# Zero fills of a decode kernel's cache gradients: the source rows, 32 partitions four apart, become 16 partitions eight apart

## Chip, cores and metric

One core of a Trainium2 chip. The time is the device time of one execution in microseconds; a kernel's figure is the median of several executions. A profile comes from one further execution, whose own time is given beside its span (first to last instruction).

## What is computed

The reference is one decode step of a transformer block, forward and backward: a layer norm, attention of one new token over the last W = 4096 positions of a key and value cache of Sk = 32768 positions, a gated bilinear feed-forward part, and the gradients of nine inputs. Cut to what matters here:

```python
def _A_ref(x, k_cache, v_cache, wq, wo):
    B, Sq, D = x.shape                       # 1, 1, 448
    Hq, Dh = 16, 256
    Hkv, Sk = k_cache.shape[1], k_cache.shape[2]   # 8, 32768
    W = min(4096, max(256, Sk // 4))         # 4096
    q = (x @ wq).reshape(B, Sq, Hq, Dh) ...
    k = jnp.repeat(k_cache[:, :, Sk - W:, :], rep, axis=1)
    v = jnp.repeat(v_cache[:, :, Sk - W:, :], rep, axis=1)
    scores = jnp.einsum("bhqd,bhkd->bhqk", q, k) * (Dh ** -0.5)
    p = _softmax(scores, axis=-1)
    o = jnp.einsum("bhqk,bhkd->bhqd", p, v)
    ...

x = A_x
h = x + _A_ref(_layernorm(x, axis=-1), A_k_cache, A_v_cache, A_wq, A_wo)
h2 = h + _B_ref(_layernorm(h, axis=-1), B_w_gate, B_w_up, B_w_down)

_out, _vjp = jax.vjp(_f, A_x, A_k_cache, A_v_cache, A_wq, A_wo, B_w_gate, B_w_up, B_w_down)
_grads = _vjp(grad_out)
```

The two largest outputs are the gradients of the caches, `out_2` and `out_3`, each (1, 8, 32768, 256) in bf16. Only the last 4096 positions of a head have a gradient; the first 28672 are zeros, and they have to be written. These zeros are 16 regions (8 heads, K and V) of 14336 KB.

## The kernel before

**Zeros.** Each region is written by one DMA out of SBUF, called a fill, which reads the same zeroed rows again and again. `rows_of(src, n)` takes every fourth partition of a tile, 32 rows in all, and repeats each n times by a stride of zero (line 244). A fill's destination is cut into 32 equal stretches, one for each row.

- The two *early* fills (lines 254 and 255) read `Z_early`, which is the tile `pair`, cleared by a memset at the start (line 71): 32 KB a row, 28 times. SyncE issues them behind the first loads, which it also issues (lines 122, 123 and 212 to 217): the projection weights, K and V of the first three heads and V of head 3. GpSimd waits for both fills (line 256) before V of heads 5 and 6 is loaded into `pair`.
- The fourteen *late* fills read `Z_late`, which is the tile `home`: 16 KB a row, NZ = 28 times. `home` is at first V of head 0 (line 67). When head 0's part of the forward pass has read it, `clear_rows` (line 289) zeroes every fourth partition by one AND with a mask that is 0 in the rows to be cleared and all ones in the others (`keep_i`, built in lines 148 to 152 from an identity matrix). The 96 other partitions keep V of head 0 for the backward pass.
- `fill_late` (line 261) issues the late fills on SyncE's queue `ZQ`, two in flight (DEEP = 2): before a fill SyncE waits for the one two places earlier. After the last it waits for all (lines 284 to 287).
- The fill of region 3 (UNEVEN) is cut: 22 of the 28 repeats go as usual; the last 192 pieces of 16 KB go in six small transfers that start from given rows (line 275), four of them issued by GpSimd.

**The rest.** The forward pass goes head by head (`scores`, then `moments`, lines 401 to 414), with loads of later heads on ScalarE's queue `LD`. Then come the output projection and the feed-forward part with their gradients (lines 432 to 570). The backward pass goes through the heads in the order 6, 1, 3, 4, 5, 0, 7, 2 (line 669): per head it reads V, builds 2 MB each of K's and V's gradient in SBUF and stores both on ScalarE's queue (line 712), while GpSimd computes and stores the weight gradients.

In the third round of that loop (it == 2) all of `home` is copied into another place by VectorE (line 714), and the 32 partitions that had been cleared are loaded again from the cache (line 715), so that the copy holds V of head 0 whole for the round of head 0.

## Time and profile before

| | us |
|---|---|
| median of three runs (784.61 to 786.02) | 785.4 |
| profiled execution | 784.5 |
| its span, first to last instruction | 782.7 |
| PE busy | 474.3 |
| DVE busy | 386.1 |
| ACT busy | 197.9 |
| POOL busy | 189.9 |

PE is the matrix engine TensorE, DVE is VectorE, ACT ScalarE, POOL GpSimd, SP SyncE. Transfers run on 16 DMA engines, which serve all queues: q1 is SyncE's, q10 ScalarE's, q0 GpSimd's. The page gives each queue's packets, bytes in MB and the time of its packets as a share of 16 engines' span. The mean granted TensorE clock of the execution was 0.766 of full speed.

### The profile page before, as it was taken

What the parts mean: (1) busy time and instruction counts of PE and PEld (TensorE: products, weight loads), DVE (VectorE), ACT (ScalarE), POOL (GpSimd) and SP (SyncE); (2) the same over time, 40 slices, a digit from 0 to 9 for tenths busy, and PEclk for the clock granted to TensorE, in tenths of its full rate; (3) what the DMA queues carried; (4) which work ended last, traced back from release to release, by engine and by line L of the source; (5) the groups of instructions that cost most, each with busy time, mean ns of one, the idle gap of its engine ahead of it and who ended that gap; (6) DMA issues with size and microseconds to landing.
All of it is one profiled execution on the core that took longest, in us unless ns stands there. A gap on an engine that the chain in (4) does not pass through costs nothing.

```text
span 782.7 us, 6390 instructions
## 1 busy us (share of the span) xinstructions
PE 474.3 (61%) x2166; PEld 203.4 (26%) x2184; DVE 386.1 (49%) x1090; ACT 197.9 (25%) x309; POOL 189.9 (24%) x102
## 2 busy tenths in 40 slices
PE   1999999999689992522233598533687906502200
PEld 0444444444344441200012134211233302201000
DVE  8158545464027753104378627582468504796400
ACT  1251332323440000001011026431555503510300
POOL 7000001000000000000000096762828565590000
PEclk9999999999968996655555699955589555755555
DMA  9999999999999999999999999999999999999998
GB/s 376 430 424 428 429 432 417 424 428 428 430 430 431 423 427 427 430 430 429 432 432 428 433 429 427 427 427 412 431 426 414 425 418 430 428 432 431 429 429 353
DMA packets 23698, 331.96 MB, mean 424 GB/s; under 512 B 1774, under 2 KB 2802, under 8 KB 4946
## 3 DMA queue, kind: packets, MB, share of 16 engines
q1 hardware_dynamic: 14826, 250.43, 75.3%
q10 hardware_dynamic: 5320, 57.61, 17.4%
q0 software_dynamic: 3520, 23.51, 7.2%
q8 instruction: 17, 0.28, 0.1%
q14 instruction: 15, 0.12, 0.0%
HBM read 50.96 MB, written 280.59 MB: 424 GB/s over the span
## 4 chain that ended last, share of the span: by engine, by line
PE 41%; DMA 18%; DVE 16%; issue 3%; another core or an unknown queue 2%; ACT 2%; DVEq 0%; ACTq 0%; POOLq 0%
PE M_t L384 11%; DMA out_dram<-arena 11%; PE rows_ps L321 6%; PE tr_ps L318 6%; PE ok_ps L388 5%; PE d_ps L702 4%; DVE arena L710 2%; DVE arena L523 2%; DVE pair L729 2%; DVE arena L709 2%; DMA arena<-in_A_wo_dram 2%; DMA arena<-in_A_k_cache_dram 2%; PE dqb_ps L580 2%; DMA arena<-in_B_w_down_dram 2%
## 5 line engine op out<-in xcount | busy, mean ns | idle before, releaser
L380 DVE TENSOR_SCALAR arena<-arena,p_f 128x256 bf16<-128x256 bf16 x512 | 110.4, 282 | 38.4 <-PE M_t L384 21.0
L318 PE MATMUL tr_ps<-ident_f,arena 128*128 128x128 f32 x448 | 85.0, 318 | 58.1 <-DMA arena<-in_A_v_cache_dram 31.4
L321 PE MATMUL rows_ps<-arena,vpad 128*16 128x512 bf16 x256 | 88.1, 438 | 9.3 <-ACT arena L675 3.6
L337 ACT COPY arena<-tr_ps 128x1024 bf16<-128x1024 bf16 x64 | 63.7, 1013 | 98.5 <-PE tr_ps L318 84.6
L318 PEld LDWEIGHTS tr_ps<-ident_f,arena 128*128 128x128 f32 x448 | 55.3, 158 | 104.1 <-issue 74.5
L709 DVE CAST arena<-d_ps 128x512 bf16<-128x512 f32 x64 | 44.0, 688 | 66.0 <-PE d_ps L702 65.7
L702 PE MATMUL d_ps<-arena 32*128 32x512 bf16 x256 | 46.5, 514 | 49.1 <-DVE arena L710 41.8
L384 PE MATMUL M_t<-arena 128*128 128x512 bf16 x308 | 73.5, 380 | 1.9 <-DVE arena L380 1.5
L706 ACT CAST arena<-d_ps 128x512 bf16<-128x512 f32 x64 | 37.9, 591 | 83.3 <-PE d_ps L702 79.6
L597 POOL TENSOR_SCALAR arena<-dh_bc,oX_f 128x448 bf16<-128x448 bf16 x32 | 44.5, 1399 | 29.5 <-DMA out_dram<-arena 29.3
L710 DVE CAST arena<-d_ps 128x512 bf16<-128x512 f32 x64 | 43.5, 680 | 14.2 <-DMA out_dram<-arena 14.2
L707 ACT CAST arena<-d_ps 128x512 bf16<-128x512 f32 x64 | 38.4, 600 | 23.8 <-DMA out_dram<-arena 23.8
L388 PE MATMUL ok_ps<-arena 128*32 128x512 bf16 x208 | 43.3, 380 | 0.3 <-issue 0.3
L417 POOL DMA_DIRECT2D arena<-in_A_wo_dram x1 | 0.6, 569 | 166.3 <-PE ok_ps L388 166.3
L675 ACT COPY arena<-tr_ps 128x1024 bf16<-128x1024 bf16 x32 | 32.6, 1024 | 28.9 <-PE rows_ps L321 19.3
L384 PEld LDWEIGHTS <-arena 128*128 128x128 bf16 x320 | 29.7, 98 | 36.5 <-issue 4.3
L597 POOL TENSOR_SCALAR arena<-arena,xT 128x4096 bf16<-128x4096 bf16 x3 | 31.8, 10615 | 26.3 <-DMA out_dram<-arena 26.3
L477 PE MATMUL r_ps<-arena,X2pad 128*4 128x448 bf16 x24 | 10.4, 570 | 39.6 <-DMA arena<-in_B_w_up_dram 23.4
L702 PEld LDWEIGHTS <-arena 32*128 32x128 bf16 x256 | 10.4, 96 | 87.2 <-DVE arena L710 43.9
L597 POOL TENSOR_SCALAR arena<-pair,xT 128x1792 bf16<-128x1792 bf16 x6 | 28.7, 4791 | 12.8 <-DMA out_dram<-arena 12.8
L323 DVE COPY arena<-rows_ps 16x512 f32<-16x512 f32 x16 | 10.8, 677 | 42.5 <-PE rows_ps L321 42.3
L384 PE MATMUL M_t<-arena,pair 128*128 128x512 bf16 x124 | 30.2, 404 | 0.4 <-issue 0.2
(237 smaller groups left out, 589.8 us busy)
## 6 DMA issues: line engine op xcount, KB each, us to landing
out_dram<-home SPq DMA_DIRECT2D x13, 14336.0 KB, 89.4
out_dram<-arena ACTq DMA_DIRECT2D x16, 2048.0 KB, 27.8
out_dram<-pair SPq DMA_DIRECT2D x2, 14336.0 KB, 90.5
out_dram<-home SPq DMA_DIRECT2D x1, 11264.0 KB
arena<-in_A_k_cache_dram ACTq DMA_DIRECT2D x5, 2048.0 KB, 19.1
arena<-in_A_k_cache_dram SPq DMA_DIRECT2D x3, 2048.0 KB, 24.4
arena<-in_A_v_cache_dram SPq DMA_DIRECT2D x3, 2048.0 KB, 29.7
arena<-in_A_v_cache_dram ACTq DMA_DIRECT2D x3, 2048.0 KB, 33.5
```

Source lines behind the costliest of these rows:

```text
L318: nc.tensor.transpose(tr_ps[:, i, :], X_sb[:, 4 * q + i, :].bitcast(f32), ident_f[:])
L321: nc.tensor.matmul(rows_ps[:], lhsT=pad[:, e, 16 * q:16 * q + 16], rhs=XT.rearrange("p (n e) -> p n e", e=2)[:, :, e], start=(q == 0 and e ...
L337: sT_ps = dots(K_of[g], KT_slot, vpad[g % 2], rows1, ps_c, "cols", lambda q, XT, ps: nc.scalar.copy(out=XT, in_=ps))
L380: nc.vector.tensor_scalar(out=pK[:, i, hh, :], in0=K_sb[:, t, :], scalar1=p_f[:, 8 * i + c, hh:hh + 1], scalar2=None, op0=ALU.mult)
L384: nc.tensor.matmul(M_ps[vh], lhsT=V_sb[:, t, vh * 128:(vh + 1) * 128], rhs=pK[:, i, :, :].rearrange("p h d -> p (h d)"), start=(t == 0), s ...
L388: nc.tensor.matmul(ok_ps[32 * k:32 * (k + 1), :], lhsT=ppad[g % 2][:, t:t + 2, :].rearrange("p t h -> p (t h)"), rhs=X_sb[:, t:t + 2, :].r ...
L597: nc.gpsimd.tensor_scalar(out=buf[:, off:off + n], in0=src, scalar1=col, scalar2=None, op0=ALU.mult)
L702: nc.tensor.matmul(d_ps[:, qi].rearrange("p w d -> p (w d)"), lhsT=rm[32 * q:32 * (q + 1), l, :], rhs=Rs[32 * q:32 * (q + 1), :], start=Tr ...
L706: nc.scalar.copy(out=stV[:, t:t + 2, :], in_=d_ps[:, :, 0, :])
L707: nc.scalar.copy(out=stK[:, t:t + 2, :], in_=d_ps[:, :, 1, :])
L709: nc.vector.tensor_copy(out=stV[:, t:t + 2, :], in_=d_ps[:, :, 0, :])
L710: nc.vector.tensor_copy(out=stK[:, t:t + 2, :], in_=d_ps[:, :, 1, :])
```

## The change

The number of rows becomes a constant, ZP = 16, and their distance ZS = 128 // ZP = 8. All fills read partitions 0, 8, 16 ... 120 in place of 0, 4, 8 ... 124, and each row is repeated twice as often: NZ is 56, and the early fills repeat 56 / 2 = 28 times over 16 rows of 32 KB each with stretches twice as long. The mask clears 16 partitions of `home` and keeps 112; the reload of line 715 fetches 16 rows in place of 32. The six small transfers keep their pieces and start from rows of the new set.

```diff
-NZ = (Sk - W) * Dh // (32 * ZW)
+ZP = 16
+ZS = 128 // ZP
+NZ = (Sk - W) * Dh // (ZP * ZW)
...
-    nc.vector.reduce_sum(out=keep_f[:], in_=ident_f[:, 0:128:4], axis=AX)
+    nc.vector.reduce_sum(out=keep_f[:], in_=ident_f[:, 0:128:ZS], axis=AX)
...
-        return src[0:128:4].unsqueeze(1).to_broadcast([32, n, src.shape[1]])
+        return src[0:128:ZS].unsqueeze(1).to_broadcast([ZP, n, src.shape[1]])
...
-        fill_with(reg.rearrange("(p n f) -> p n f", p=32, f=ZE), rows_of(Z_early, NZ * ZW // ZE), esem, "early")
+        fill_with(reg.rearrange("(p n f) -> p n f", p=ZP, f=ZE), rows_of(Z_early, NZ * ZW // ZE), esem, "early")
...
-                odd = reg.rearrange("(r f) -> r f", f=ZW)[22 * 32:]
-                reg = reg[0:22 * 32 * ZW]
-                n = 22
+                odd = reg.rearrange("(r f) -> r f", f=ZW)[44 * ZP:]
+                reg = reg[0:44 * ZP * ZW]
+                n = 44
                 at = 0
-                for e, base, rows, queue in ((3, 0, 8, nc.gpsimd), (2, 12, 2, nc.gpsimd), (3, 20, 13, nc.gpsimd), (8, 64, 13, nc.gpsimd), (4, 0, 5, ZQ), (1, 0, 1, ZQ)):
+                for e, base, rows, queue in ((3, 0, 8, nc.gpsimd), (2, 3, 2, nc.gpsimd), (3, 5, 13, nc.gpsimd), (8, 8, 13, nc.gpsimd), (4, 0, 5, ZQ), (1, 0, 1, ZQ)):
                     fill_with(odd[at:at + e * rows].rearrange("(e n) f -> e n f", e=e),
-                              Z_late[base:base + 4 * e:4].unsqueeze(1).to_broadcast([e, rows, ZW]), zsem[j] if queue is ZQ else psem, "fills", queue)
+                              Z_late[ZS * base:ZS * (base + e):ZS].unsqueeze(1).to_broadcast([e, rows, ZW]), zsem[j] if queue is ZQ else psem, "fills", queue)
...
-            for dst, src in [(reg.rearrange("(p n f) -> p n f", p=32, f=ZW), rows_of(Z_late, n))]:
+            for dst, src in [(reg.rearrange("(p n f) -> p n f", p=ZP, f=ZW), rows_of(Z_late, n))]:
...
-                LD.dma_start(out=ar(S[3], 16 * KB)[0:128:4], in_=A_v_cache[0, 0, Sk - W:, :].rearrange("(p t) d -> p (t d)", t=T)[0:128:4])
+                LD.dma_start(out=ar(S[3], 16 * KB)[0:128:ZS], in_=A_v_cache[0, 0, Sk - W:, :].rearrange("(p t) d -> p (t d)", t=T)[0:128:ZS])
```

## The prediction

> **What bounds the kernel now.** I read the slices of the page first, then the queues and the DMA issues, then what SyncE and the other engines wait for, then windows of single stages, and last the chain.

> The slices over the span (DMA: mean busy share of 16 DMA engines in tenths; GB/s: what they moved):
> ```profile
> DMA  9999999999999999999999999999999999999998
> GB/s 376 430 424 428 429 432 417 424 428 428 430 430 431 423 427 427 430 430 429 432 432 428 433 429 427 427 427 412 431 426 414 425 418 430 428 432 431 429 429 353
> DMA packets 23698, 331.96 MB, mean 424 GB/s; under 512 B 1774, under 2 KB 2802, under 8 KB 4946
> ```
> The DMA engines are full from the first slice to the last: the time is bytes over rate, 331.96 MB at 424 GB/s being 782.9 us against a span of 782.7. The compute engines live inside that (PE is busy 61%).

> The queues and the issues of the fills:
> ```profile
> q1 hardware_dynamic: 14826, 250.43, 75.3%
> ...
> HBM read 50.96 MB, written 280.59 MB: 424 GB/s over the span
> ...
> out_dram<-home SPq DMA_DIRECT2D x13, 14336.0 KB, 89.4
> out_dram<-arena ACTq DMA_DIRECT2D x16, 2048.0 KB, 27.8
> out_dram<-pair SPq DMA_DIRECT2D x2, 14336.0 KB, 90.5
> ```
> q1 is SyncE's queue. The sixteen fills are 16 x 14336 KB = 234.9 MB of the 332. One engine moves on q1 250.43 MB / (0.753 x 782.7 us x 16) = 26.56 GB/s, so a 16 KB piece of a fill takes 617 ns and all fills cost 234.9 MB / (16 x 26.56 GB/s) = 552.7 us of the 782.7. The other 230 us are loads and stores.

> Who waits for the fills (engine, line, what it waited for: us in total, times, longest):
> ```profile
> SPq L247 <- DMA out_dram<-home: 555.9, 12, 71.6
> SPq L286 <- DMA out_dram<-home: 98.2, 2, 54.2
> ```
> SyncE always has two fills in flight and waits for the older; its last wait ends the program. So the pace of a fill is the pace of the kernel.

> Windows of three stages (start and end, length, busy time of PE, PEld, DVE, ACT, POOL, granted clock, DMA share, GB/s): loads alone, then almost only a fill, then fills with stores:
> ```profile
> 5.00:40.00 35.00, 21.75 (x95) 10.26 (x95) 15.04 (x29) 7.49 (x9) 10.38 (x5) 1.00 1.00 428
> 210.00:250.00 40.00, 33.48 (x128) 15.57 (x131) 17.75 (x76) 9.29 (x16) 0.00 (x0) 0.74 1.00 429
> 700.00:750.00 50.00, 8.60 (x48) 3.05 (x48) 27.30 (x40) 9.32 (x17) 4.47 (x2) 0.50 1.01 430
> ```
> Loads read HBM and write 128 partitions, fills read 32 partitions and write HBM, and both stop at the same 428 to 430 GB/s. The ceiling is therefore on what they share: the DMA engines, or the doors between these engines and SBUF.

> **The change, part by part.** *Instructions.* Every fill keeps its 14336 KB, its 16 KB pieces (32 KB for the two early ones) and their number, 896 or 448; SyncE still issues once per fill. The sum that makes the mask (line 149) reads 16 columns instead of 32; it took 200 ns once, so under 0.2 us, beside full DMA. The AND of line 291 and the copy of line 714 keep their shape. Nothing here is moved past a queue and no wait is added.

> *The reload of head 0* (line 715, ScalarE's queue) falls from 512 to 256 KB. 0.262 MB at 424 GB/s is 0.62 us of all DMA engines: -0.6 us, since the engines are never idle. It is issued at 530.49, just ahead of the two stores of line 712, which land that much sooner too.

> *The pace of a fill.* This is the whole question. Now 32 partitions give 429 GB/s in the fill-only window, 13.4 GB/s each on average; afterwards 16 must give 26.8 each, or the fill slows. No row of the trace has an SBUF side narrower than those 32 rows that runs long enough by itself. Lower bound of the cost: the engines alone are the ceiling and a piece stays at 617 ns, 0 us. Upper bound: the ceiling is at the doors, a door belongs to a set of partitions, and half of the doors are no longer used; two engines then share one door, a piece takes 2 x 617 = 1234 ns while both fill, a fill runs at 234.9 MB / 1105.4 us = 212 GB/s and all fills cost up to 552.7 us more. I take the upper price: it is a row's measured pace per source partition kept as it is, while the lower one needs every source row to give twice what any row shows it giving.

> [...]

> *What of the doubled cost is hidden.* While one engine of a pair moves a load, its partner has the door alone. At the one end both engines turn to loads and stores together, nothing overlaps, and the span is 782.7 + 552.7 - 0.6 = 1334.8 us. At the other end the shared doors are never idle: 17,920 KB (18.35 MB) of loads stand ahead of the first fill on q1, 18.35 MB / 428 GB/s = 42.9 us; then the fills take 2 x 552.7 = 1105.4; and the stores, 280.59 - 234.9 = 45.7 MB, leave through the same doors, 45.7 / 424 = 107.8 us. Together 1256.1. I take the middle, 1295.5, as the loads of a head come to all sixteen engines at once and the alternation of two queues lets part of them slip in between.

> *What else would be late.* The wait of POOL (line 256) for both early fills moves from 127 us to about 43 + 4 x 34.5 = 181, and V of heads 5 and 6 is loaded that much later; K, V and weight loads share their engines with slower pieces. The chain says how much compute hangs on transfers:
> ```profile
> PE 41%; DMA 18%; DVE 16%; issue 3%; another core or an unknown queue 2%; ACT 2%; DVEq 0%; ACTq 0%; POOLq 0%
> ```
> Even if the 18% (141 us) doubled and 54 us came on top for POOL, compute would be through at some 980 us, under fills that last to 1256 or more. So this costs nothing, and the last 300 us would be fills alone.

> *Sum.* 782.7 - 0.6 + 513.4 (the middle of 474.0, which is 1256.1 - 782.1, and 552.7) = 1295.5 us of span. The profiled execution took 784.5 us, 1.8 around its span, and the median of the runs is 785.4, 0.9 above it: 1298 us.

> **The rivals.**
> *Not slower: the engines are the ceiling.* One mechanism: a door can give two engines their 26.56 GB/s at the same time, so any 16 rows are as good as 32. It decides from the point where a door gives 53 GB/s. Then only the reload is left: 784.8 us (785.4 - 0.6). For it: each engine shows the same pace whatever queue or direction it serves. Against it: that pace is equally what a door of one engine's width would give, and the change asks the rows for something no stage has asked.
> [...]

> *Fewer engines.* The sixteen rows are dealt to eight engines only, which then carry all fills: 2 x 552.7 for these, and their 229 us of other traffic in series, 1334.8 + 2.7 = 1337 us. The busy share of DMA would fall to about 5 tenths once compute is through. Against it: the reading of 32 rows fills all sixteen now, and sixteen rows leave one for each.

> *A door with some room to spare.* If it gives a pair one and a half engines' pace, a piece costs 4/3: 552.7 / 3 = 184 more, 782.7 + 184 + 2.1 = 969 us. Against it: nothing in the slices shows a rate above 433.

> **How the numbers follow.** Shared doors 0.76, engines the ceiling 0.13, eight engines 0.06, some room 0.05. The measurement tells about 0.2% (1.6 us) from no change; the 0.6 us of the second case lies below that, so of its 0.13 I give 0.11 to the same and 0.02 to faster. Slower has the rest, 0.87. The time is that of the likeliest, 1298. The range holds the first and the third case: from 1180 (the 1256 + 2.7 of perfect overlap, less 6% if a shared door gives a little more than one engine's pace) to 1370 (1337 and 2.5% for what sharing loses). The two cases below it, 0.18 together, are left out; the end at 784.8 belongs to one of them.

> **What would show it.** In the changed profile: GB/s of the slices near 212 wherever only fills run, thus in the last quarter above all, with the DMA share still at 9 (pieces take longer, the engines don't rest); the loads-only first slices unchanged at about 428; SyncE's wait at line 247 near twice 556; fills landing some 140 us after issue in place of 89.4 where nothing else runs; compute over by 980 us and the end with SyncE's wait at line 286. A GB/s row that stays near 424 with a span near 782 makes the forecast wrong, and the engines the ceiling; a DMA share of 5 in the tail means eight engines; slices near 320 mean room to spare.

## The result and the profile after

The changed kernel takes 1416.5 us (median of 6 runs, 1414.2 to 1421.5) against 784.9 beside it: 1.804 times as long, 95% interval 1.802 to 1.807. The direction and the mechanism came as forecast, the size did not: 1298 was said, with 1370 as the upper end.

The slices over the changed kernel's span (one slice is now 35.3 us), and its queues and issues:

```profile
span 1412.4 us, 6390 instructions
...
PE   4999764895302136832272600510200000000000
...
DMA  9999999999999999999999889966994999999991
GB/s 399 285 264 258 287 342 310 204 260 324 226 224 224 245 205 204 230 256 233 253 218 264 278 275 202 223 228 193 226 249 123 201 205 203 204 204 202 206 201 55
...
q1 hardware_dynamic: 14826, 250.43, 75.3%
q10 hardware_dynamic: 5304, 57.35, 12.7%
q0 software_dynamic: 3520, 23.51, 5.7%
...
out_dram<-home SPq DMA_DIRECT2D x13, 14336.0 KB, 145.6
out_dram<-arena ACTq DMA_DIRECT2D x16, 2048.0 KB, 70.7
out_dram<-pair SPq DMA_DIRECT2D x2, 14336.0 KB, 140.4
```

The reader is to see four things. The number of packets and bytes on q1 is the same to the last digit, so the transfers are the same ones. The DMA row stays at 9 over most of the span while GB/s falls to 204 wherever nothing but fills is left: the engines are busy, each piece takes longer. Against the forecast, the DMA row does not stay at 9 everywhere: slices 23 to 31 and the last one have holes. And a 2 MB store of a head's gradient lands after 70.7 us in place of 27.8.

Windows of the changed kernel (columns as before): loads alone, then fills alone.

```profile
5.00:40.00 35.00, 21.91 (x99) 10.59 (x99) 15.01 (x29) 8.11 (x9) 10.38 (x5) 1.00 1.01 429
1105.00:1365.00 260.00, 0.00 (x0) 0.00 (x0) 0.00 (x0) 0.00 (x0) 0.00 (x0) 0.50 0.99 204
```

Loads are untouched at 429 GB/s. Fills run at 204 with all engines busy (0.99), 12.75 GB/s for each engine, so a 16 KB piece takes 1285 ns against 617 before.

SyncE's waits (what for, us in total, times, longest) say the same of whole fills:

```profile
SPq L249 <- DMA out_dram<-home: 1110.5, 12, 159.7
SPq L288 <- DMA out_dram<-home: 108.5, 2, 71.5
```

Line 249 is line 247 of before; the 555.9 us have become 1110.5, twice as much within 0.2%.

**Where the 629.7 us of span went.** The share of each queue in sixteen engines' span, times the span, is engine time. Beside q1's 75.3% the page of before gives:

```profile
q10 hardware_dynamic: 5320, 57.61, 17.4%
q0 software_dynamic: 3520, 23.51, 7.2%
```

| engine time, us | before | after | more |
|---|---|---|---|
| q1: fills and first loads | 589.4 | 1063.5 | 474 |
| q10: ScalarE's loads and stores | 136.2 | 179.4 | 43 |
| q0: GpSimd's loads and stores | 56.4 | 80.5 | 24 |
| no packet at all (span less the shares) | under 1 | 88 | 88 |

q8, which carries instructions, has 0.1% on both sides. The time without a packet is called dry time below.

### The profile page after: what moved, and what is told of

It reads as the page before. It is cut to its first block, busy times and chain, and to the rows that moved or that the text cites. A ratio compares the mean times of both kernels' runs of the same rounds, so it can differ in the third digit from the quotient of the medians.

```text
span 1412.4 us, 6390 instructions
## 1 busy us (share of the span) xinstructions
PE 488.3 (35%) x2166; PEld 208.2 (15%) x2184; DVE 396.6 (28%) x1090; ACT 198.3 (14%) x309; POOL 191.6 (14%) x102
## 3 DMA queue, kind: packets, MB, share of 16 engines
q1 hardware_dynamic: 14826, 250.43, 75.3%
HBM read 50.69 MB, written 280.59 MB: 235 GB/s over the span
## 4 chain that ended last, share of the span: by engine, by line
PE 24%; DMA 21%; another core or an unknown queue 15%; DVE 9%; issue 2%; ACT 1%; SPq 0%; DVEq 0%; ACTq 0%; POOLq 0%
DMA out_dram<-arena 9%; PE M_t L386 6%; DMA arena<-in_A_k_cache_dram 5%; PE tr_ps L320 4%; PE rows_ps L323 4%; PE ok_ps L390 3%; PE d_ps L704 2%; DMA arena<-in_B_w_down_dram 2%; DMA arena<-in_A_v_cache_dram 1%; DVE pair L731 1%; DMA arena<-in_B_w_up_dram 1%; DMA arena<-in_A_wo_dram 1%; DVE arena L711 1%; DVE arena L712 1%
## 5 line engine op out<-in xcount | busy, mean ns | idle before, releaser
L320 PE MATMUL tr_ps<-ident_f,arena 128*128 128x128 f32 x448 | 89.3, 331 | 136.9 <-DMA arena<-in_A_v_cache_dram 95.9
L599 POOL TENSOR_SCALAR arena<-arena,xT 128x4096 bf16<-128x4096 bf16 x3 | 35.7, 11888 | 54.3 <-DMA out_dram<-arena 54.3
L679 DVE COPY arena<-tr_ps 128x1024 bf16<-128x1024 bf16 x32 | 22.5, 704 | 14.4 <-PE tr_ps L320 14.0
## 6 DMA issues: line engine op xcount, KB each, us to landing
out_dram<-home SPq DMA_DIRECT2D x13, 14336.0 KB, 145.6
out_dram<-arena ACTq DMA_DIRECT2D x16, 2048.0 KB, 70.7
out_dram<-pair SPq DMA_DIRECT2D x2, 14336.0 KB, 140.4
arena<-in_A_k_cache_dram ACTq DMA_DIRECT2D x5, 2048.0 KB, 32.3
arena<-in_A_k_cache_dram SPq DMA_DIRECT2D x3, 2048.0 KB, 24.1
arena<-in_A_v_cache_dram SPq DMA_DIRECT2D x3, 2048.0 KB, 29.6
arena<-in_A_v_cache_dram ACTq DMA_DIRECT2D x3, 2048.0 KB, 53.0
```

The costliest lines, as they stand in the source:

```text
L320: nc.tensor.transpose(tr_ps[:, i, :], X_sb[:, 4 * q + i, :].bitcast(f32), ident_f[:])
L599: nc.gpsimd.tensor_scalar(out=buf[:, off:off + n], in0=src, scalar1=col, scalar2=None, op0=ALU.mult)
```

## The experiments

**Sixteen rows, 32 to 92 by four.** The changed kernel with rows counted from Z0:

```diff
-ZS = 128 // ZP
+Z0 = 32
+ZS = 4
+ZR = slice(Z0, Z0 + ZP * ZS, ZS)
...
-    nc.vector.reduce_sum(out=keep_f[:], in_=ident_f[:, 0:128:ZS], axis=AX)
+    nc.vector.reduce_sum(out=keep_f[:], in_=ident_f[:, ZR], axis=AX)
...
-        return src[0:128:ZS].unsqueeze(1).to_broadcast([ZP, n, src.shape[1]])
+        return src[ZR].unsqueeze(1).to_broadcast([ZP, n, src.shape[1]])
...
-... Z_late[ZS * base:ZS * (base + e):ZS] ...
+... Z_late[Z0 + ZS * base:Z0 + ZS * (base + e):ZS] ...
...
-LD.dma_start(out=ar(S[3], 16 * KB)[0:128:ZS], in_=...[0:128:ZS])
+LD.dma_start(out=ar(S[3], 16 * KB)[ZR], in_=...[ZR])
```

> Sixteen rows as in the changed kernel, but partitions 32, 36 ... 92 in place of 0, 8 ... 120. Shared doors (two engines read through one door when their rows lie 32 apart, and rows that differ in their place within 32 or lie on the two sides of 64 have doors of their own): every engine has a door for itself, 611 to 617 ns a piece, 424 GB/s, about 784 us, that is the kernel before less the 0.6 us of the reload. Number of rows (a partition hands out no more than 13 to 14 GB/s): as slow as the changed kernel, about 1412 us.

784.8 us against 785.5 beside it, ratio 0.9993 (0.9984 to 1.0002). A window with almost only a fill:

```profile
210.00:250.00 40.00, 33.11 (x153) 15.74 (x156) 18.77 (x81) 10.25 (x18) 0.00 (x0) 0.88 1.01 431
```

Sixteen rows give 431 GB/s, each of them 27. That ends the rival of the number of rows, and any that says sixteen rows are narrow: only where they lie differs from the changed kernel. The destinations and their sixteen stretches are the same too, so the loss is not on the side of HBM.

**Sixteen rows, 0 to 60 by four.** As above with Z0 = 0.

> Sixteen rows, partitions 0, 4 ... 60: the same count and spacing as rows 32 to 92, but every row has a partner 32 away. Shared doors: a piece at 1220 to 1280 ns, fills alone at about 204 GB/s, 1330 to 1420 us. Spacing (rows eight apart are the trouble, four apart are not): about 784 us. Number of rows: about 1412 us, the same as shared doors; the run with rows 32 to 92 tells these two apart.

1323.7 us, ratio 1.685 (1.681 to 1.689), a little below the range of shared doors. Same count, same spacing, 32 partitions lower, and the pace is half. Its fills alone, in the last quarter of the slices:

```profile
DMA  9999999999999999999999999979978999999994
GB/s 399 306 252 280 257 305 342 258 202 298 307 223 225 225 243 203 204 226 262 240 291 242 276 342 263 256 279 298 235 253 210 206 204 201 204 204 205 200 204 189
```

204 GB/s again. Spacing is out: what rows 32 to 92 have and these do not is rows on both sides of partition 64. Near the end the trace shows the sharing itself:

```profile
1295.00:1315.00 20.00, 0.00 (x0) 0.00 (x0) 0.00 (x0) 0.00 (x0) 0.00 (x0) 0.50 0.50 215
```

Half of the engines have ended (0.50), and the others move 215 GB/s, more than all sixteen did: 27 for each engine instead of 12.75, as if each now had a door to itself.

**Thirty-two rows, 0 to 62 by two.** ZP = 32, Z0 = 0, ZS = 2, 28 repeats, with the cut fill of region 3 as in the kernel before.

> Thirty-two rows as in the kernel before, but partitions 0, 2 ... 62, which by the door theory lie at eight doors. Shared doors: fills at half pace, 1330 to 1420 us. Number of rows: as before, about 785 us.

1330.3 us, ratio 1.694 (1.690 to 1.697), though the number of rows is that of the kernel before. Fills alone, and the queues:

```profile
1120.00:1290.00 170.00, 0.00 (x0) 0.00 (x0) 0.00 (x0) 0.00 (x0) 0.00 (x0) 0.50 0.99 205
...
q1 hardware_dynamic: 14826, 250.43, 81.3%
q10 hardware_dynamic: 5320, 57.61, 11.5%
q0 software_dynamic: 3520, 23.51, 5.7%
```

With q8's 0.1% the shares leave 1.4% of 1328.0 us, so only some 19 us are dry here.

**Sixteen rows, 0 to 15.** Z0 = 0, ZS = 1.

> Sixteen rows side by side, partitions 0 to 15, in groups of four that have one door. Shared doors: four engines to a door, a piece at 2440 to 2560 ns, fills alone at some 102 GB/s, 2250 to 2600 us. If a fixed cost of narrow sources were the cause (half pace whatever the rows, unless they are spread as 32 to 92): about 1330 to 1412 us.

2459.2 us, a single run. Fills alone:

```profile
1700.00:2400.00 700.00, 0.00 (x0) 0.00 (x0) 0.00 (x0) 0.00 (x0) 0.00 (x0) 0.50 0.99 102
```

Half of 204 with all engines busy: 2570 ns a piece, four times 617 within 5%. The cost does not follow the number of rows: sixteen of them gave 431, 204 and 102 GB/s, thirty-two 429 and 205. At the 26.9 GB/s that each of the last eight engines moved with rows 0 to 60 (215 / 8), sixteen, eight and four doors would give 430, 215 and 108. So I count sixteen, eight and four doors, a shared one at 25.5 GB/s (204 / 8 and 102 / 4); the count is read off the paces. What the expectation for rows 32 to 92 says of doors fits rows four apart: no sharing between places within 32 or between the two sides of 64 (431 GB/s), sharing once every row has a partner 32 away (204). Rows two apart and side by side share beyond that (205 and 102), so a place within 32 is not always a door of its own.

**The reload by itself.** In the kernel before:

```diff
-LD.dma_start(out=ar(S[3], 16 * KB)[0:128:4], in_=...[0:128:4])
+LD.dma_start(out=ar(S[3], 16 * KB)[0:128:8], in_=...[0:128:8])
```

> The kernel before with the reload of head 0's values cut from 32 to 16 rows (0, 8 ... 120), so sixteen cleared rows stay zeros in the copy and the gradients that use them are left wrong. This is the saving of the change by itself: 0.262 MB at 424 GB/s is 0.6 us, 784.8 in place of 785.4, a ratio of 0.999. If the reload lay on a chain of its own and not only on the DMA engines, more than 2 us would go.

784.7 against 785.5, ratio 0.9988 (0.9979 to 0.9997). The interval ends just below one, so a small gain is likely; the 0.9992 of 0.6 us lies in it and in that of rows 32 to 92 (0.9993), and the intervals are too wide to say more.

**The early fills alone.** In the kernel before, where an early fill repeats its 32 KB rows 14 times (not 28, as its description ahead has it), 28 times after the edit:

```diff
-        fill_with(reg.rearrange("(p n f) -> p n f", p=32, f=ZE), rows_of(Z_early, NZ * ZW // ZE), esem, "early")
+        fill_with(reg.rearrange("(p n f) -> p n f", p=16, f=ZE), Z_early[0:128:8].unsqueeze(1).to_broadcast([16, NZ * ZW // ZE * 2, ZE]), esem, "early")
```

> The kernel before, with the two early fills alone reading sixteen rows eight apart; the fourteen late ones and the reload stay. Shared doors: 2 of 16 fills at half pace, 552.7 x 2/16 = 69 us at most, less what loads hide in the first 180 us: 840 to 855 us. If the late load of two heads' values (GpSimd's wait for the early fills) stopped the forward pass beyond that, over 860; if the half pace came only from the tile the late fills read, 785.

841.6 us, ratio 1.073 (1.070 to 1.075). The slices (21 us each) and GpSimd's wait:

```profile
GB/s 382 427 267 210 293 273 238 288 301 399 429 429 429 424 429 427 427 429 431 430 434 427 436 428 425 428 429 416 428 417 429 415 428 430 431 432 427 428 428 337
...
POOL pair L210 <- POOLq L256: 177.7, 1, 177.7
```

The slower pace is there as long as the early fills run (down to 210 GB/s in the fourth slice) and gone with them (429 from the eleventh on). They cost 56.8 us of the 69.1 that two doubled fills would cost with nothing hidden, so 12 us (18%) slipped in between loads. GpSimd waits 177.7 us for them in place of 111.8, and nothing comes of it: later slices are back at the rates of before.

**Four fills in flight.** In the changed kernel, to find the 88 us without packets:

```diff
-DEEP = 2
+DEEP = 4
```

> The changed kernel with four fills in flight instead of two. In the changed kernel the packets fill 93.8% of sixteen engines' span, so 1324 us of work and 88 us without any. Theory: engines fall out of step, and SyncE issues the next fill only when the slowest engine has ended the one two places earlier, so the fast ones run dry. Then four in flight take away the dry stretch about 1060 to 1100 us and part of the tail: 1330 to 1385 us. Rival: some engines simply have more work at their doors, so that they end late whatever is queued: within 10 us of 1412, the dry time only moved to the end.

1421.6 us, ratio 1.8125 to the kernel before (1.809 to 1.816): no gain. My theory fell, the rival held. The slices:

```profile
DMA  9999999999999999999999998898849999999921
GB/s 400 284 263 256 293 333 313 204 259 328 222 225 226 241 203 204 232 259 231 252 225 275 270 259 245 211 263 258 270 117 205 204 203 205 203 204 203 198 51 47
```

The tail is longer: two slices (71 us) at about 50 GB/s, and the shares of the queues leave 102 us dry in place of 88. A window in this tail, and one in that of the changed kernel:

```profile
1350.00:1400.00 50.00, 0.00 (x0) 0.00 (x0) 0.00 (x0) 0.00 (x0) 0.00 (x0) 0.50 0.25 51
...
1380.00:1410.00 30.00, 0.00 (x0) 0.00 (x0) 0.00 (x0) 0.00 (x0) 0.00 (x0) 0.50 0.13 54
```

Here four engines (0.25 of 16) are left with 51 GB/s, 12.75 each, the half pace, as two shared doors at 25.5 would give. In the changed kernel two are left with 54, 27 each, the full pace. So some engines end late with four fills in flight as with two; that with two part of this shows earlier, as SyncE waiting for the slowest, fits the holes but is not shown.

**Without the heads' stores.** In the changed kernel:

```diff
-            for o_ap, st_ in ((out_3, stV), (out_2, stK)):
-                LD.dma_start(out=o_ap[0, g, Sk - W:, :].rearrange("(p t) d -> p t d", t=T), in_=st_)
```

> The changed kernel without the sixteen 2 MB stores of the heads' gradients (33.6 MB, left unwritten). Theory: these stores leave through the same doors and put the engines out of step; without them 33.6 MB / 16 / 26.56 GB/s = 79 us of engine time go and most of the 88 dry us with them, 1245 to 1285 us. Rival (they do not matter for the dry time): 79 us at most, 1330 us or more, with DMA slices below 9 as before.

1239.0 us, ratio 1.579 (1.576 to 1.582) to the kernel before, 177 us less than the changed kernel, a little below the range given. The slices and queues:

```profile
DMA  9999999999999999999999999999999999999994
...
q1 hardware_dynamic: 14826, 250.43, 86.9%
q0 software_dynamic: 3520, 23.51, 6.7%
q10 hardware_dynamic: 3000, 23.79, 4.6%
```

With 98.3% of the span in packets (q8's 0.1% counted), 21 us are dry in place of 88, and the holes in the DMA row are gone but for the last slice. So 67 of the 88 dry us need the stores. That these put the engines out of step, by leaving SBUF through doors that fills use, is the likely reason, not a shown one; and the stores do not do it alone, as rows 0 to 62 keep them and have only 19 us dry. The rest of the 175 us of span is engine time, 108 us, more than the 79 of the stores at full pace. Which engines fall behind, and why two or four of them, the trace does not say, as its packets carry no engine; that stays open.

## Why the prediction was right and wrong

**The bound.** Bytes over rate, and the fill as the pace of the kernel: right. Among what loads and fills share, the prediction left out HBM. The windows near the ends settle that: two engines move 54 GB/s, eight 215 and sixteen 429 to 431, 27 for each in all these windows, so the ceiling goes with the single engine, or with a door that has one engine at it, and no limit common to all sixteen shows. SyncE's wait doubled as said (1111 against "near twice 556"), fills land after 140 to 146 us ("some 140").

**The pace of a fill.** The upper price was right. Its reason, "half of the doors are no longer used", was my estimate, as no run then read fewer than 32 rows for long by itself; the paces agree with it, 431 GB/s for rows 32 to 92 against 204, 205 and 102 for 0 to 60, 0 to 62 and 0 to 15. The other reason I gave beside it, that the lower price "needs every source row to give twice what any row shows it giving", was false: sixteen rows in the right places give exactly that. It stood beside the right reason and proved nothing.

**What the trace could not tell.** Against rival "fewer engines", the DMA share is 0.99 with fills alone, not 5 tenths. "The engines are the ceiling" and "some room to spare" fell with the 204 GB/s.

**The size: the step that failed.** *What of the doubled cost is hidden* put everything between 1256 and 1335 us of span, on the ground that "the engines don't rest". Packets alone fill 1324 us in the changed kernel, inside those bounds; what broke them is 88 us in which engines have nothing to do. The sum had no such term, and its upper end, all work in series, assumed that all sixteen engines end together. Without the heads' stores the dry time is 21 us. The stores stood in my sum as 107.8 us at the doors, but only for the end at which the doors never rest, not as something that holds some engines up more than others. The dry time also hangs on which rows share: with rows 0 to 60 it is some 43 us (the shares leave 3.3% of 1323.8), with rows 0 to 62 some 19 of 1328.0, and both spans lie inside the bounds, near the upper end. Why engines drift apart most with the rows of the changed kernel stays open.

**A smaller term.** Sharing loses some 4% here: fills alone run at 204 GB/s where 212 was worked out, so all fills at that pace are 234.9 MB / 204 GB/s = 1151 us, 599 more than before, and all work in series would be 782.7 + 599 - 0.6 = 1381 us, still short of 1412. For the 232.1 MB of fills on q1 (the rest is GpSimd's pieces on q0) it is 592 more. The q1 row shows 474 more, so 118 us slipped in beside loads and stores, while q10 and q0 took 43 + 24 = 67 us more themselves, a price I had set at nothing. The 6% and the 2.5% at the ends of the range were my estimates; no run shows either, and two engines that share moved 25.5 GB/s against the 26.56 worked out for one.

**Late work.** "Compute would be through at some 980 us" was some 40 us early: the last slice with PE work ends at 1024 us. It hid beneath the fills all the same, and GpSimd's later wait cost nothing, as the early fills alone show.

**The reload.** -0.6 us stands, within what the runs can tell.

## What to carry to other kernels

When a transfer bounds a kernel, ask where its rows lie, not only how many there are: here sixteen rows, 32 to 92 by four, ran as fast as thirty-two, 0 to 124 by four (784.8 us against 785.5), and thirty-two rows, 0 to 62 by two, as slowly as sixteen, 0 to 60 by four (1330.3 against 1323.7). If the rows must be few, try several places for them and look at GB/s with the DMA share beside it: busy engines (0.99) at half the rate (204 against 429 GB/s) were the mark of sharing here. In a bound of the form "all work in series", leave room for engines that do not end together (88 us in the changed kernel).

## What was not expected

Sharing was nearly exact over a factor of four (431, 204, 102 GB/s), so none of these doors had pace to spare beyond one engine's (25.5 GB/s shared, 26.9 for one engine). And ordinary stores beside the slow fills cost far more than their bytes: 33.6 MB, 79 us of engine time at full pace, were worth 175 us of span in the changed kernel. Rows 32 to 92 by four take the change's price away (784.8 us); against the kernel before that is no difference the runs can tell.
